# A transformer block on one Trainium2 core: two full expert pairs found among the first four batches and run beside the routing of the rest

## The chip, the cores and the metric

The kernel runs on one core of one Trainium2 chip. The metric is the device time of one execution in microseconds (us), the median of several; lower is better.

## The reference

Three stages, all in float32. Attention without a softmax on 8 batches, 8 heads, 576 tokens, head size 64; then a mixture of 8 experts that sends each of the 4608 tokens to its best expert; then a gated linear unit. Cut to its core:

```python
kv = np.einsum('bhsd,bhse->bhde', k, v)
out = np.einsum('bhsd,bhde->bhse', q, kv)
rms = np.sqrt(np.mean(out * out, axis=-1, keepdims=True) + 1e-06)
x = (out / rms * g_norm)                      # as tokens x 512
logits = x @ w_gate + modality_bias[modality_id]
e_idx = np.argmax(logits, axis=1)             # gate_w: softmax of the logits at e_idx
for e in range(8):                            # w1[e]: 512 x 1024, w2[e]: 1024 x 512
    mask = e_idx == e
    h = np.maximum(x[mask] @ w1[e], 0.0)
    out[mask] = gate_w[mask, None] * (h @ w2[e])
gate = 1.0 / (1.0 + np.exp(-(out @ w_gate2)))  # 512 x 1536
result = (gate * (out @ w_val)) @ w_out        # 1536 x 512
```

## The kernel before, in words

Every engine runs its instructions in the order in which the program emits them; the order is written out by hand. PE multiplies, DVE and ACT evaluate and split, POOL issues gathers and scatters, SP issues the other transfers. Float32 products are done as three products of split operands: ACT rounds a tile to a high part (`hi`), DVE subtracts it to get the residue (`lo`).

**Attention.** A loop over b = 0 to 8 (L397) computes batch b's `kv` products (`emit_kv`, into the matrix R) and transposed queries while it finishes batch b-1, in five steps r (`emit_out`, L290: the products of 128 tokens each, whose rows ACT copies and squares and whose squares DVE sums, L305). For b-2 it runs `norm` (L307: root mean square, and the logits). Batches go to the routing in pairs: `choose` (L330) takes the best expert, `rank` (L344) gives each token its place among the tokens of its expert, by ten small matmuls (L352 to L355) and a running total `tot` (L350), `lanes` (L371) and `numbers` (L378) make the one-hot tiles `lid` that carry token numbers, on POOL for the first two pairs of batches and on ACT (L385) for the others. `store_x` (L389) writes a batch's rows to `x_d` in DRAM through SP.

**Routing.** After the loop come the last `norm`, `choose`, `rank` and `lanes`, and then, on L478 to L548, the table of the whole: each expert's tokens are counted, cut into pair items of 256 tokens (18 of them) and single items of 128, and for each slot of 128 tokens the kernel finds the code (`sc`, L503), the token numbers by one-hot matmuls (`soh`, `php`, L508 to L520, giving `gidx`), the expert of each item (`est`, L524 to L531, which SP reads into registers) and the rows where results go (`sidx`, L533 to L548).

**Experts.** `run` (L925) goes through items 0 to 21, four steps each (j, a quarter of the hidden columns). A step: `emit_B` (24 matmuls with w1), the split of the next w1 quarter (`split_w`, L737), `emit_h` (ReLU and residue, L802 and L803), the split of the w2 quarter, `emit_D` of the step before (12 matmuls with w2). `gather` (L724) fetches the rows of an item from `x_d` by `gidx`, `norm_x` (L753) scales them, `emit_A` (L761) transposes them. Items alternate between two halves of a weight buffer; the pieces of item t+2 are loaded on SP as the pieces of item t have been split, under a register that skips the load where the expert is the same as two items before. Items 0 and 1 begin with expert 0, loaded ahead (L412, L451, L934, L935). `emit_y` (L839) scatters an item's result to `y_d`. `run` also unpacks float64 weights of the last stage (`Decode`, 28 units of 512 KB), one every 2.5 steps (L851), each loaded two steps before ACT takes its exponent (L129).

**The gated unit** (L1000 on) reads `y_d` and is bound by PE throughout. Its tiles `wos` (L1112) and `yr` (L1170) lie in pools of its own.

Of the kernel before, what the change touches and what calls it, by code (L numbers as in the profile page):

```python
# [1 line left out]

# [19 lines left out]
NT = B * S  # L22
# [11 lines left out]
NITEM = NPAIR + E  # L34
KC = DM // 128
# [47 lines left out]
def attention_moe_glu_kernel(  # L83
# [18 lines left out]
    est = const.tile([1, 2 * NITEM + 1], I32, name="est")  # L102

# [7 lines left out]
    class Decode:  # L111
# [34 lines left out]
        def store(self):  # L146
            m, cb, c = self.m, self.cb, self.c
            if m < 2:
                lo = (0, 128, 256, 384, 768, 896, 512, 640)[4 * m + c]
                nc.sync.dma_start(out=w_d[cb][:, :, lo:lo + 128], in_=self.f.rearrange("p (j f) -> p j f", f=128))  # L150
            else:
                nc.sync.dma_start(out=w_d[cb][:, c, 1024:1536], in_=self.f)

# [5 lines left out]
    with ExitStack() as st:  # L159
# [130 lines left out]
        def emit_out(b, r):  # L290
            if r == 0:
                o_t[b] = wk.tile([128, 4 + b % 2, XW], F32, tag=f"o{b % 2}", name="o", bufs=4 - b % 2)
# [85 lines left out]
        def numbers(bp, lo, act):  # L378

            t0, n, bc = 9 * bp, 9, [128, 9, 128]  # L380
            for w in range(2):
# [14 lines left out]

        for b in range(B + 1):  # L397
# [6 lines left out]
            for r in range(5):  # L404
                if b == B and r == 0:
# [4 lines left out]
                    w1r = [half0[:, 0].rearrange("p (c f) -> p c f", f=F1)]  # L410
                    w2r = [half0[:, 1].rearrange("p (c f) -> p c f", f=DM)]
                    nc.sync.dma_start(out=w1r[0], in_=w1[0].rearrange("(c p) f -> p c f", p=128))  # L412
# [15 lines left out]
                if r == 1:  # L428
# [6 lines left out]
                    for i in {6: (0, 1, 2), 7: (3, 4)}.get(b, ()):  # L435
                        store_x(i)
# [12 lines left out]
        norm(B - 1)  # L449
        store_x(B - 1)  # L450
        nc.sync.dma_start(out=w2r[0], in_=w2[0].rearrange("(c p) f -> p c f", p=128))  # L451
        numbers(2, lo, True)
        choose(3)
        lane = rank(3)


        tp = pkv.tile([128, 16], F32, tag="kv", name="totp")
        nc.tensor.matmul(out=tp[:, 0:8], lhsT=onesb, rhs=tot[:, 4, :], start=True, stop=True)
        for i in range(E):
            nc.tensor.matmul(out=tp[:, 8 + i:9 + i], lhsT=onesb, rhs=tot[:, 4, E - 1 - i:E - i], start=True, stop=True)  # L460
        numbers(3, lanes(3, lane), True)
        w1s = {(0, 0): [w1p.tile([128, KC, 256], F32R, tag="w1" + z, name="w1" + z) for z in "hl"]}
        wq = w1r[0][:, :, 0:256]
        nc.scalar.activation(out=w1s[0, 0][0], in_=wq, func=ACTF.Copy)
# [11 lines left out]
        soh = big.tile([128, NTILE, NSLOT], BF16, name="soh")  # L476
        item = ct[:, C_ITEM:C_ITEM + NITEM]
        nc.vector.tensor_scalar(out=ti, in0=tp, scalar1=127.0, scalar2=None, op0=ALU.add)  # L478
        nc.vector.tensor_scalar(out=ti, in0=ti, scalar1=7, scalar2=None, op0=ALU.arith_shift_right)
        nc.vector.tensor_scalar(out=tw[:, 0::2], in0=ti.rearrange("p (a e) -> p a e", a=2), scalar1=-2, scalar2=None, op0=ALU.bitwise_and)  # L480

        nc.vector.tensor_scalar(out=tw[:, 0, 0:1], in0=tw[:, 0, 0:1], scalar1=2.0, scalar2=None, op0=ALU.max)
        nc.vector.tensor_scalar(out=tw[:, 2, 7:8], in0=tw[:, 2, 7:8], scalar1=2.0, scalar2=None, op0=ALU.max)
        nc.vector.tensor_tensor(out=tw[:, 1], in0=ti[:, 8:16], in1=tw[:, 2], op=ALU.subtract)
        nc.vector.tensor_scalar(out=cums[0][:, :, 4:12], in0=tw[:, 0:2], scalar1=0.0, scalar2=None, op0=ALU.max)
        for i in range(3):
            nc.vector.tensor_tensor(out=cums[i + 1][:, :, 4:12], in0=cums[i][:, :, 4:12], in1=cums[i][:, :, 4 - 2 ** i:12 - 2 ** i], op=ALU.add)

        nc.vector.tensor_copy(out=seg[:, 0:9], in_=cums[3][:, 0, 3:12])
        nc.vector.tensor_scalar(out=seg[:, 9:10], in0=cums[3][:, 0, 11:12], scalar1=float(2 * NPAIR), scalar2=None, op0=ALU.max)  # L490
        nc.vector.tensor_scalar(out=seg[:, 10:18], in0=cums[3][:, 1, 4:12], scalar1=seg[:, 9:10], scalar2=None, op0=ALU.add)

        nc.vector.tensor_tensor(out=off, in0=ct[:, C_CODE:C_CODE + 18], in1=seg, op=ALU.subtract)
        nc.vector.tensor_tensor(out=off[:, 9:17], in0=off[:, 9:17], in1=tw[:, 2], op=ALU.add)
        nc.vector.tensor_tensor(out=dlt, in0=off[:, 1:18], in1=off[:, 0:17], op=ALU.subtract)
        bc = [128, NITEM, 17]
        nc.vector.tensor_tensor(out=cmp, in0=seg[:, 1:18].unsqueeze(1).broadcast_to(bc), in1=item.unsqueeze(2).broadcast_to(bc), op=ALU.is_le)
        nc.vector.tensor_tensor(out=cm2, in0=cmp, in1=dlt.unsqueeze(1).broadcast_to(bc), op=ALU.mult)
        nc.vector.tensor_reduce(out=itc, in_=cm2, op=ALU.add, axis=AX)
# [183 lines left out]
    with ExitStack() as st:  # L683
# [40 lines left out]
        def gather(t):  # L724
            if t >= end:
                return
# [605 lines left out]
```

## Time and profile before

| | |
|---|---|
| median of 3 runs | 1491.02 us (1490.17 to 1494.47) |
| profiled execution | 1496.44 us, its span 1494.7 us |
| mean granted clock of PE | 0.984 |
| PE, DVE, ACT, POOL busy, share of the span | 96%, 61%, 43%, 15% |
| HBM | 311.27 MB read, 68.63 MB written |

The span runs from the first to the last instruction on the core; the execution's own time has the launch around it. A busy PE counts pipelined matmuls, so durations of neighbouring matmuls overlap and the distance between their starts is the better price. A row of a timeline gives start and duration in us; "idle before" names what ended the wait. The granted clock is a share of full speed, 2.4 GHz.

### The profile page before, as it was taken

The page shows a single profiled execution, that of the slowest core. Times are in us where ns is not written, and L with a number is a line of the kernel's source. Part 1 is how long each engine was busy: PE and PEld are TensorE (multiplying, and loading weights), DVE is VectorE, ACT ScalarE, POOL GpSimd, SP SyncE. Part 2 cuts the span into 40 slices and gives each one's busy share as a digit, 9 for nine tenths or more (in the row PEclk, how much of TensorE's full clock was granted, in tenths as well). Part 3 has the DMA queues.
Part 4 walks back from the last instruction along what each step waited for, and adds up shares of the span by engine and source line. Part 5 has one row for each costly group of instructions (what it writes and reads, how often), then busy time and mean ns, then how long its engine had stood idle before and what let it go on. Part 6 is the DMA issues. An engine that isn't in the chain of part 4 may idle for free.

```text
span 1494.7 us, 22909 instructions
## 1 busy us (share of the span) xinstructions
PE 1429.6 (96%) x8633; PEld 1225.2 (82%) x8633; DVE 909.2 (61%) x1402; ACT 638.9 (43%) x1005; POOL 228.6 (15%) x302
## 2 busy tenths in 40 slices
PE   6984799999999999999999999999999999999997
PEld 6974689999999998778888887888888888888886
DVE  2557778788888877647876676343653436444442
ACT  3656455555555556746433342232322323221221
POOL 1011222222222221311011101010010200101011
PEclk9998799999999999999999999999999999999999
DMA  9975798858886766859886666556474564646444
GB/s 297 345 288 211 215 267 289 276 173 276 293 286 208 241 194 207 295 190 351 321 336 246 247 239 232 212 194 249 156 260 185 217 227 173 242 167 236 176 159 157
DMA packets 154979, 356.31 MB, mean 238 GB/s; under 512 B 20592, under 2 KB 74096, under 8 KB 147696
## 3 DMA queue, kind: packets, MB, share of 16 engines
q1 hardware_dynamic: 141872, 317.03, 61.0%
q0 software_dynamic: 11488, 36.27, 7.1%
q8 instruction: 71, 1.16, 0.3%
q10 hardware_dynamic: 1504, 1.48, 0.3%
q14 instruction: 44, 0.36, 0.1%
HBM read 311.27 MB, written 68.63 MB: 254 GB/s over the span
## 4 chain that ended last, share of the span: by engine, by line
PE 55%; DMA 1%; issue 0%; DVE 0%; POOL 0%; ACT 0%; POOLq 0%
PE gv L646 10%; PE gv L648 10%; PE gv L647 10%; PE ac L1163 6%; PE ac L1161 6%; PE ac L1162 6%; PE gv L620 1%; PE gv L621 1%; PE gv L622 1%; PE tr L583 1%; DMA wt_d<-wt 1%; POOL out_dram L1145 0%; DVE u L650 0%; POOLq L1328 0%; DVE wt L609 0%
## 5 line engine op out<-in xcount | busy, mean ns | idle before, releaser
L650 DVE TENSOR_TENSOR gm<-u,gv 128x512 f32<-128x512 f32 x96 | 65.9, 687 | 173.5 <-PE gv L648 172.3
L1161 PE MATMUL ac<-wos,gh 128*128 128x512 f32 x432 | 168.7, 390 | 0.0
L1163 PE MATMUL ac<-wos,gl 128*128 128x512 f32 x432 | 168.6, 390 | 0.0
L1162 PE MATMUL ac<-wos,gh 128*128 128x512 f32 x432 | 168.1, 389 | 0.0
L788 PE MATMUL ph<-xh,w1h 128*128 128x256 f32 x576 | 166.8, 290 | 0.8 <-ACT xh L771 0.8
L789 PE MATMUL ph<-xh,w1l 128*128 128x256 f32 x576 | 164.0, 285 | 1.2 <-DVE w1l L750 1.2
L790 PE MATMUL ph<-xl,w1h 128*128 128x256 f32 x576 | 164.1, 285 | 0.0
L670 ACT ACTIVATE s<-gv 128x512 f32<-128x512 f32 x48 | 28.8, 600 | 265.2 <-issue 207.7
L835 PE MATMUL py<-w2h,hh 128*128 128x512 f32 x304 | 119.3, 392 | 0.0
L836 PE MATMUL py<-w2l,hh 128*128 128x512 f32 x304 | 119.3, 392 | 0.0
L837 PE MATMUL py<-w2h,hl 128*128 128x512 f32 x304 | 118.5, 390 | 0.0
L646 PE MATMUL gv<-half,wt 128*128 128x512 f32 x288 | 113.3, 394 | 0.6 <-DVE u L650 0.6
L789 PEld LDWEIGHTS ph<-xh,w1l 128*128 128x128 f32 x576 | 111.3, 193 | 2.7 <-DVE w1l L750 1.4
L788 PEld LDWEIGHTS ph<-xh,w1h 128*128 128x128 f32 x576 | 111.2, 193 | 2.5 <-ACT xh L771 1.2
L648 PE MATMUL gv<-half,wt 128*128 128x512 f32 x288 | 112.5, 390 | 0.0
L647 PE MATMUL gv<-half,wt 128*128 128x512 f32 x288 | 112.1, 389 | 0.0
L790 PEld LDWEIGHTS ph<-xl,w1h 128*128 128x128 f32 x576 | 111.1, 193 | 0.3 <-DVE xl L772 0.3
L650 DVE TENSOR_TENSOR s<-u,gv 128x512 f32<-128x512 f32 x48 | 33.0, 688 | 118.3 <-PE gv L648 118.2
L1145 POOL DMA_INDIRECT out_dram<-ot,to x36 | 37.1, 1029 | 439.1 <-DVE ot L1142 190.4
L1163 PEld LDWEIGHTS ac<-wos,gl 128*128 128x128 f32 x432 | 81.1, 188 | 17.9 <-DVE gl L1130 0.4
L1162 PEld LDWEIGHTS ac<-wos,gh 128*128 128x128 f32 x432 | 81.1, 188 | 17.2
L1161 PEld LDWEIGHTS ac<-wos,gh 128*128 128x128 f32 x432 | 81.1, 188 | 17.0 <-ACT gh L1129 0.2
(275 smaller groups left out, 3323.7 us busy)
## 6 DMA issues: line engine op xcount, KB each, us to landing
wt<-wt_d SPq DMA_DIRECT2D x36, 1536.0 KB
wos<-wo_d SPq DMA_DIRECT2D x96, 512.0 KB
half<-in_moe_w_dram SPq DMA_DIRECT2D x88, 512.0 KB
w1r<-in_moe_w_dram SPq DMA_DIRECT2D x44, 512.0 KB
w2r<-in_moe_w_dram SPq DMA_DIRECT2D x44, 512.0 KB
rows<-w_d SPq DMA_DIRECT2D x24, 512.0 KB
wt<-wt_d SPq DMA_DIRECT2D x48, 256.0 KB
wt_d<-wt SPq DMA_DIRECT2D x12, 1024.0 KB
```

Of the source, the lines that this page charges most:

```text
L646: nc.tensor.matmul(out=o, lhsT=wh, rhs=yh[:, c, :], start=first and c == 0, stop=False, skip_group_check=True)
L647: nc.tensor.matmul(out=o, lhsT=wh, rhs=yl[:, c, :], start=False, stop=False, skip_group_check=True)
L648: nc.tensor.matmul(out=o, lhsT=wl, rhs=yh[:, c, :], start=False, stop=last and c == 1, skip_group_check=True)
L788: nc.tensor.matmul(out=o, lhsT=bh[:, c, cs], rhs=hi[:, c, 0:n], start=(c == 0), stop=False)
L789: nc.tensor.matmul(out=o, lhsT=bl[:, c, cs], rhs=hi[:, c, 0:n], start=False, stop=False)
L790: nc.tensor.matmul(out=o, lhsT=bh[:, c, cs], rhs=lo[:, c, 0:n], start=False, stop=(c == KC - 1))
L835: nc.tensor.matmul(out=o, lhsT=hi[:, f, cs], rhs=bh[:, f, :], start=first, stop=False)
L836: nc.tensor.matmul(out=o, lhsT=hi[:, f, cs], rhs=bl[:, f, :], start=False, stop=False)
L837: nc.tensor.matmul(out=o, lhsT=lo[:, f, cs], rhs=bh[:, f, :], start=False, stop=last)
L1161: nc.tensor.matmul(out=o, lhsT=gh[:, cs], rhs=wh, start=(k == 0), stop=False)
L1162: nc.tensor.matmul(out=o, lhsT=gh[:, cs], rhs=wl, start=False, stop=False)
L1163: nc.tensor.matmul(out=o, lhsT=gl[:, cs], rhs=wh, start=False, stop=(k == NJ - 1))
```

## The change

The functions of the expert stage move to the top of the kernel, with their tiles taken from whatever pool is set in `al`; the pool of x rows (`xp`) is open for the whole kernel. Then:

- In b = 6, step 2, `front_items` counts the tokens of each expert in batches 0 to 3, takes the first two full 256s in the order of the experts (`kd`: how many of them each expert gives) and writes their experts and codes.
- In b = 7, `front_rows` finds their token numbers by 36 one-hot matmuls, then the rows are gathered and SP reads the experts.
- In b = 8 the front's rows are scaled, transposed and split beside attention's last products. Item 0's weights are loaded by expert, in 8 pieces; item 1's pieces follow into the same half, if its expert differs.
- The eight steps of the two front items are emitted with the routing of the rest cut into pieces between them (`CHAIN`); `kd` takes the front's tokens out of the table, which now gives items 2 to 21. In step 6 the rows of items 2 and 3 are gathered and item 2's weights loaded. The scatter places follow the last step.
- Front results go to consecutive rows of `y_d` by a plain transfer.
- `run` begins with item 2; item 3's weights are loaded by SP at its start. One decode unit comes every 2.25 steps.
- Batches' row tiles have one buffer less (3 and 2), so `store_x` of batches 1, 0, 3 and 2 is emitted earlier. `wos` and `yr` use the tiles of `xp`.

The diff, cut to its core (the moved functions are otherwise as before):

```diff
+        def front_items():
+            ps = pq.tile([128, 8], F32, tag="q", name="tote")
+            nc.tensor.matmul(out=ps, lhsT=onesb, rhs=tot[:, 2, :], start=True, stop=True)
...
+            nc.vector.tensor_scalar(out=fi, in0=ps, scalar1=0.0, scalar2=None, op0=ALU.add)
+            nc.vector.tensor_scalar(out=fi, in0=fi, scalar1=8, scalar2=None, op0=ALU.arith_shift_right)
+            nc.vector.tensor_scalar(out=cue[0][:, 4:12], in0=fi, scalar1=0.0, scalar2=None, op0=ALU.max)
+            for i in range(3):
+                nc.vector.tensor_tensor(out=cue[i + 1][:, 4:12], in0=cue[i][:, 4:12], in1=cue[i][:, 4 - 2 ** i:12 - 2 ** i], op=ALU.add)
+            nc.vector.tensor_scalar(out=cf, in0=cue[3][:, 3:12], scalar1=float(NFRONT), scalar2=None, op0=ALU.min)
+            nc.vector.tensor_tensor(out=kd, in0=cf[:, 1:9], in1=cf[:, 0:8], op=ALU.subtract)
...
+            nc.vector.tensor_copy(out=est0, in_=ep[0:1])
+
+        def front_rows():
...
+            nc.vector.tensor_tensor(out=se, in0=sce.unsqueeze(1).broadcast_to(bc), in1=code[:, 0:n].unsqueeze(2).broadcast_to(bc), op=ALU.is_equal)
+            ps = pq.tile([128, 2, 2 * NFRONT], F32, tag="q", name="phe")
+            for w in range(2):
+                for t in range(n):
+                    nc.tensor.matmul(out=ps[:, w, :], lhsT=lid[:, t, w, :], rhs=se[:, t, :], start=(t == 0), stop=(t == n - 1))
+            nc.vector.tensor_scalar(out=ve, in0=ps[:, 0], scalar1=128.0, scalar2=-1.0, op0=ALU.mult, op1=ALU.add)
+            nc.vector.tensor_tensor(out=gidx0, in0=ve, in1=ps[:, 1], op=ALU.add)
...
-                    nc.sync.dma_start(out=w1r[0], in_=w1[0].rearrange("(c p) f -> p c f", p=128))
+                    for j in range(NJ1):
+                        load_w(0, j, 0)
+                        load_w(0, j, 1)
...
-                    for i in {6: (0, 1, 2), 7: (3, 4)}.get(b, ()):
+                    for i in {5: (1,), 6: (0, 3, 2), 7: (4,)}.get(b, ()):
                         store_x(i)
...
+                if b == B - 2 and r == 2:
+                    front_items()
+                if b == B - 1:
+                    if r == 2:
+                        front_rows()
+                    if r == 3:
+                        for t in range(NFRONT):
+                            gather(t)
+                    if r == 4:
+                        for t in range(NFRONT):
+                            read_item(t)
+                if b == B:
+                    if r in (1, 2):
+                        norm_x(0, r - 1)
+                    if r in (2, 3):
+                        emit_A(0, r - 2)
+                    if r == 3:
+                        split_w(0, 0, 0)
+                        load_w(1, 0, 0)
+                    if r == 4:
+                        split_w(0, 1, 0)
+                        load_w(1, 1, 0)
+                        split_w(0, 0, 1)
+                        load_w(1, 0, 1)
...
+        CHAIN = {0: [norm_last], 1: [lambda: numbers(2, lo, True, (0,)), lambda: choose(3), ranks],
+                 2: [lambda: numbers(2, lo, True, (1,)), totals, lanes3], 3: [segments, lambda: numbers(3, front.lo, True, (0,))],
+                 4: [slots, lambda: numbers(3, front.lo, True, (1,))], 5: [tokens], 6: [experts]}
+        steps = [(t, j) for t in range(NFRONT) for j in range(NJ1)]
+        for s, (t, j) in enumerate(steps):
+            emit_B(t, j)
+            for do in CHAIN.get(s, ()):
+                do()
+            emit_h(t, j)
+            if s == 6:
+                al.end = NSURE
+                for i in range(2):
+                    gather(NFRONT + i)
+            nt, nj = steps[s + 1] if s + 1 < len(steps) else (NFRONT, 0)
+            if nt < NFRONT:
+                split_w(nt, nj, 0)
+                if s and nt == 0:
+                    load_w(1, nj, 0)
+            split_w(t, j, 1)
+            if s and t == 0:
+                load_w(1, j, 1)
+            if s == 6:
+                for i in range(2):
+                    read_item(NFRONT + i)
+                for q in range(NJ1):
+                    load_w(NFRONT, q, 0)
+                    if q <= j:
+                        load_w(NFRONT, q, 1)
+            if s:
+                emit_D(*steps[s - 1])
+                if steps[s - 1][1] == NJ1 - 1:
+                    emit_y(steps[s - 1][0])
+            if t == 0:
+                if j in (0, 1):
+                    norm_x(1, j)
+                if j in (1, 2):
+                    emit_A(1, j - 1)
+        load_w(NFRONT, NJ1 - 1, 1)
+        for i in range(2):
+            norm_x(NFRONT, i)
+        split_w(NFRONT, 0, 0)
+        emit_D(*steps[-1])
+        for i in range(2):
+            emit_A(NFRONT, i)
+        emit_y(NFRONT - 1)
+        places()
...
-                at.setdefault((5 * i // 2 + d, what), []).append(i)
+                at.setdefault((9 * i // 4 + d, what), []).append(i)
...
-        run(0, NSURE)
+        run(NFRONT, NSURE)
```

## Rows read from the trace of the kernel before

**Rows 1.** The page, part 1: busy time, share, instructions of each engine.

```profile
PE 1429.6 (96%) x8633; PEld 1225.2 (82%) x8633; DVE 909.2 (61%) x1402; ACT 638.9 (43%) x1005; POOL 228.6 (15%) x302
```

**Rows 2.** Windows of 10 us: busy us (instructions), granted clock, DMA share, GB/s.

```profile
90.00:100.00 10.00, 6.56 (x142) 6.02 (x143) 5.08 (x17) 5.07 (x10) 1.36 (x3) 1.00 1.07 377
...
130.00:140.00 10.00, 1.69 (x21) 1.30 (x20) 8.82 (x29) 5.45 (x14) 0.21 (x1) 0.77 0.95 354
140.00:150.00 10.00, 0.90 (x19) 0.79 (x19) 8.97 (x38) 7.94 (x28) 0.22 (x1) 0.50 0.79 272
150.00:160.00 10.00, 2.80 (x72) 2.67 (x71) 9.08 (x34) 3.88 (x8) 3.38 (x4) 0.50 0.41 136
160.00:170.00 10.00, 8.34 (x37) 7.37 (x38) 4.25 (x6) 2.65 (x4) 4.59 (x5) 0.52 0.89 296
```

**Rows 3.** Timeline of PE: start, us, line, output<-inputs, count, idle before and its releaser.

```profile
122.57 1.23 PE L299 MATMUL ops<-R,qT 128*128 128x144 f32 x8
...
131.41 1.20 PE L299 MATMUL ops<-R,qT 128*64 128x144 f32 x16 [0.92 <-ACT o L301]
...
151.89 2.80 PE L512 MATMUL php<-soh,lid 128*128 128x44 bf16 x72 [8.42 <-DVE soh L508]
160.88 2.12 PE L767 MATMUL xtp<-ident,xg 128*128 128x128 f32 x8 [6.20 <-DVE sidx L548]
163.78 0.58 PE L788 MATMUL ph<-xh,w1h 128*128 128x256 f32 x1 [0.78 <-ACT xh L771]
...
212.08 0.28 PE L788 MATMUL ph<-xh,w1h 128*128 128x256 f32 x1
...
217.70 0.28 PE L788 MATMUL ph<-xh,w1h 128*128 128x256 f32 x1
```

**Rows 4.** Timeline of DVE around the routing.

```profile
110.71 0.17 DVE L350 TENSOR_TENSOR tot<-tot,tr 128x8 bf16<-128x8 bf16 x1
...
125.68 0.21 DVE L280 COPY R<-mp 128x64 f32<-128x64 f32 x1
...
130.38 0.17 DVE L314 TENSOR_SCALAR ssq<-ssq 128x32 f32<-128x32 f32 x1
...
138.07 0.18 DVE L314 TENSOR_SCALAR ssq<-ssq 128x40 f32<-128x40 f32 x1
...
142.55 0.28 DVE L349 TENSOR_REDUCE tr<-oh 128x8 f32<-128x72 bf16 x1
...
145.73 0.17 DVE L478 TENSOR_SCALAR ti<-totp 128x16 int32<-128x16 f32 x1
...
148.67 0.61 DVE L497 TENSOR_TENSOR cmp<-seg,ct 128x442 f32<-128x442 f32 x1
...
151.27 2.02 DVE L508 TENSOR_TENSOR soh<-sc,code 128x396 bf16<-128x396 bf16 x4
...
155.33 0.59 DVE L524 TENSOR_REDUCE esf<-cmp 1x26 f32<-1x442 f32 x1
...
157.02 0.44 DVE L533 TENSOR_TENSOR ex<-lg,mx 128x288 f32<-128x288 f32 x1
...
160.14 0.69 DVE L759 TENSOR_TENSOR xg<-xg 128x512 f32<-128x512 f32 x1
```

**Rows 5.** Groups of DVE, 220 to 600 us: busy us, mean ns, idle before.

```profile
L803 DVE SCALAR_TENSOR_TENSOR hl<-ph,hh 128x512 fp32r<-128x512 f32 x63 | 43.3, 688 | 25.2 <-ACT hh L802 25.2
L750 DVE TENSOR_TENSOR w1l<-half,w1h 128x1024 fp32r<-128x1024 f32 x34 | 41.5, 1222 | 2.5 <-ACT w1h L749 2.5
...
L772 DVE SCALAR_TENSOR_TENSOR xl<-xtp,gcol,xh 128x512 fp32r<-128x512 f32 x32 | 24.0, 751 | 24.7 <-ACT xh L771 21.0 <-issue 3.7
L759 DVE TENSOR_TENSOR xg<-xg 128x512 f32<-128x512 f32 x31 | 21.2, 684 | 0.0
```

**Rows 6.** Timeline of ACT: the lane products and a late decode piece.

```profile
138.43 5.35 ACT L385 ACTIVATE lid<-lo,ct 128x128 bf16<-128x128 bf16 x18
...
196.90 0.67 ACT L129 ACTIVATE d_e<-d_raw 128x512 f32<-128x512 f32 x1 [3.20 <-DMA d_raw<-in_moe_w_gate_dram]
```

More of the change, by code (lines that the diff above doesn't have):

```diff
@@ new lines, in part, with source, load_w @@
+    def part(t, j, which):
+        half = t % 2 if t >= NFRONT else 0
+        if which == 0:
+            return w1r[half][:, :, j * 256:j * 256 + 256]
+        return w2r[half][:, 2 * j:2 * j + 2, :]
+    def source(e, j, which):
+        if which == 0:
+            src = w1[bass.ds(e, 1), :, j * 256:j * 256 + 256]
+        else:
+            src = w2[bass.ds(e, 1), j * 256:j * 256 + 256, :]
+        return src.rearrange("o (c p) f -> p (o c) f", p=128)
+    def load_w(t, j, which):
+        if t < min(al.end, NSURE):
+            e, new = regs[t]
+            when = {} if new is None else dict(cond=new, cond_hint=False)
+            nc.sync.dma_start(out=part(t, j, which), in_=source(e, j, which), **when)
@@ new lines, in load_piece, with gather @@
+    def load_piece(t, j, which):
+        p = dec.tile([128, 1024], F32, tag="d_raw", name="d_raw", bufs=4)
+        src = source(regs[t][0], j, which)
+        p = p.rearrange("p (c f) -> p c f", f=src.shape[2])
+        nc.sync.dma_start(out=p, in_=src)
+        return p
+    xg_t, xT_t, hT_t, w2s, py_t = {}, {}, {}, {}, {}
+    def gather(t):
+        if t >= al.end:
+            return
+        for i in range(tiles_of(t)):
+            k = first_slot(t) + i
+            x = xp.tile([128, XW], F32, tag="xg", name="xg", bufs=4)
+            src, idx = (x_d[0:NT // 2, :], gidx0) if t < NFRONT else (x_d[:, :], gidx)
+            nc.gpsimd.indirect_dma_start(out=x, out_offset=None, in_=src,
+                                         in_offset=bass.IndirectOffsetOnAxis(ap=idx[:, k:k + 1], axis=0))
+            xg_t[t, i] = x
@@ new lines, in plain, with split_w @@
+    def plain(t, j, which=1):
+        return t >= NPAIR and which == 1 and j % 2 == 1
+    def split_w(t, j, which):
+        if t >= al.end or (t, j) in (w1s, w2s)[which]:
+            return
+        dst = (w1s, w2s)[which]
+        nm = f"w{which + 1}"
+        shape = [128, KC, 256] if which == 0 else [128, 2, DM]
+        src = load_piece(t, j, which) if t >= NSURE else part(t, j, which)
+        if plain(t, j, which):
+            dst[t, j] = (src, None)
+            return
+        hi, lo = al.w2() if which else [w1p.tile(shape, F32R, tag=nm + z, name=nm + z, bufs=3) for z in "hl"]
+        nc.scalar.activation(out=hi, in_=src, func=ACTF.Copy)
+        nc.vector.tensor_tensor(out=lo, in0=src, in1=hi, op=ALU.subtract)
+        dst[t, j] = (hi, lo)
@@ L496, in attention_moe_glu_kernel @@
[L496 to L499, printed above, removed]
-        nc.vector.scalar_tensor_tensor(out=itc, in0=itc, scalar=ct[:, C_CODE:C_CODE + 1], in1=item, op0=ALU.add, op1=ALU.add)
-        pairs = sc[:, 0:2 * NPAIR].rearrange("p (t i) -> p t i", i=2)
@@ L544, in attention_moe_glu_kernel, with ranks @@
[L544 to L548 removed]
+        def ranks():
+            front.lane = rank(3)
```

483 lines of the change are left out of this document (253 added, 230 removed).

## Prediction

> **What bounds the kernel now.** I read the page's totals first: PE is busy 1429.6 us of the span of 1494.7 [rows 1], so an edit pays only where PE stands still or is slow. The windows show where: from 130 to 160 us PE is busy 1.69, 0.90 and 2.80 us while DVE is busy 8.8 to 9.1, and the granted clock falls to 0.50, which is 1.2 GHz of the two levels [rows 2]. PE's timeline gives the edges: attention's last products run at 131.41 (1.20 us), the first transposes of gathered tokens at 160.88, the first expert product at 163.78 [rows 3]. Thus 31 us pass with hardly any PE work. DVE's timeline says what fills them: one unbroken chain, from batch 6's norm at 130.38, through norm and choice (138.07), rank and lanes (142.55), totals and segments (145.73), slots (148.67), one-hots (151.27), experts (155.33) and scatter places (157.02), to the first use of gathered tokens at 160.14 [rows 4]. The routing is serial work of small instructions on DVE, and the experts wait for all of it.
>
> **The yardstick.** Call T the moment at which the second product block of item 2 begins; by then both kernels have done the same expert work, items 0 and 1 whole and one block of item 2. It is 217.70 before [rows 3]. Behind it PE is full, so what T gains the end should gain. F is the moment of the first expert product, 163.78 before.
>
> **What comes first: does it find its pairs?** The reference's own arithmetic on its default inputs gives 442, 187, 206, 364, 209, 236, 367 and 293 tokens for the experts in batches 0 to 3. Experts 0, 3, 6 and 7 have full 256s, so the front items are expert 0 and expert 3. Over all batches there are still 18 pairs and 4 singles: no expert work is added. But items 2 and 3 are expert 0 again, in both halves, so its weights come twice more: I count 20 weight sets of 4 MB in place of 18.
>
> **F, step by step.** *Batch 6 of the loop.* The count of the front is a matmul behind rank's totals, ready at 110.88 [rows 4]; PE, in order, holds the next outputs and kv(7) behind it, about 1.4 us. Its 18 small DVE instructions cost (148.67 - 145.73) / 16 = 0.18 us each [rows 4], 3.3 us. DVE is not full there, so the copy that ends R of batch 7, at 125.68 [rows 4], moves by between 0 and 4.7 (3.3 + 1.4); I take 1.2, since DVE then mostly waits for PE's kv products: 126.9.
> *Batch 7.* The front's rows need a comparison (0.25), 36 matmuls and two additions (0.4). 72 such matmuls took 2.80 [rows 3], so 36 take 1.4; with the hand-overs the table stands at 129.5. They sit in PE's queue ahead of output (6,3), which began at 122.57 [rows 3] and now begins at 129.0. Two transposed tiles and two more outputs lie between it and batch 6's norm, 6.5 us by PE and ACT: norm at 135.5 in place of 130.38, 5.1 late (bounds: nothing, if PE's order hid it, and the 6.4 by which output (6,3) is late). This is the part of the change that costs.
> *The tail of attention.* Norm and rank take 4.6 (130.38 onwards, as the like of them at 138.07 and 142.55 do [rows 4]): 140.1. Then DVE has two sums of squares (512 columns like the scaling's, 0.7 each), lanes (1.3 of the 3.2 from 142.55 to 145.73), and, new, two scalings of gathered rows (0.68), two residues of x (0.75) and one of w1 (1.22) [rows 5], with 1.2 of waiting for ACT: 148.1. F is 148, 15.8 us before the old one. Without any of the delays of batches 6 and 7 it would be 142, with all of them at their upper bound 151.
>
> **From F to T.** A step of the expert pipeline (24 products, 12 second products) takes 217.70 - 212.08 = 5.62 us of PE [rows 3]. Nine first blocks and eight second ones are 8 x 5.62 + 2.85 = 47.8; four groups of transposes at 0.5 are 2.0; the routing's matmuls 2.8 + 0.9: 53.5. On DVE a step costs two residues of weights (1.22 each), one of h (0.69) and, in two steps of four, a scaling and a residue of x: 3.1 to 4.5 [rows 5]. The chain adds to steps 0 to 6 its pieces of 3.1, 3.2, 1.9, 3.0, 2.6, 2.6 and 1.7, and places (3.1) at the end [rows 4]. In steps 3 to 6 that makes 4.8 to 6.1, about what PE takes; in step 1 it is 7.7. Going through the queues in their order I find PE waiting five times: 2.8 for rank (the second block ends at F + 5.8, the choice at F + 8.5), 0.6 and 0.8 for split weights in steps 3 and 4, 1.3 for the residue of x ahead of item 2, 1.4 for places ahead of the next residue. That is 6.9: T = F + 60.4 = 208.4. ACT's lane products (5.35 per 18 [rows 6]) are spread at 2.7 over steps 1 to 4, where ACT has no more than its share of three copies and a transposed tile besides, and I let them fit.
> The gain is 217.70 - 208.4 = 9.3. Two more hand-overs of the kind that hl shows (25.2 / 63 = 0.4 [rows 5]) I take off: 8.5.
> PE's rate at F: the windows from 140 on, nearly empty, have 0.50, and the one from 90 to 100 us, with 6.56 busy, has 1.00 [rows 2]. PE before F is about half busy, so the first block may run at 1.2 GHz, 2.8 us more; PE waits 2.8 for rank right behind it, so it costs nothing.
>
> **What else moves, at nothing.** The conditional loads of item 1 sit in SP's queue ahead of the stores of batches 5 to 7; these are wanted only by the gather in step 6, some 35 us on, and the 4 MB of stores need 11 us at the 354 GB/s of [rows 2]. Item 3's weights (4 MB) queue on SP behind item 2's and ahead of the first decode piece, where POOL issued them before; they are due three steps later, 17 us against some 12. Decode pieces at every 2.25 steps in place of 2.5 add 0.1 us or so of DVE to a step with over 0.8 to spare. Later tiles that move to the pool of x rotate as before. Cover gone, each of these shows as a PE wait of some us at items 2 to 5.
>
> **Rivals.** *The routing hides better* (0.2). If DVE's slack takes the table of the front and PE's waits are half of mine, F is 144 and T 144 + 57 = 201: 17 gained, 1474. For it: DVE idles before 125, with 5.08 of 10 busy at 90 [rows 2]; against it: PE's order in batch 7.
> *Late transfers* (0.15). ACT waited 3.20 for a decode piece at 196.90 [rows 6], and the windows carry up to 377 GB/s [rows 2]. Items 2 and 3 now ask for 8 MB of weights beside some 3 MB of rows and decode in 23 us of PE, more than that rate gives; the 2 to 3 MB over take 7 us. If those fall on PE, 1 to 3 remain: 1489.
> *The queues serialise, slower* (0.11). Place: steps 0 to 7. If each piece of the chain adds its whole time to its step, since h waits on DVE behind a piece that waits for PE, T = F + 53.5 + 21.2 + 1.3 = 224.0: 6.3 lost, 1497. It decides once DVE has over 5.6 us in every step; by my sums it does in one or two. The Trainium skill (PSUM — Partial Sum Buffer, Engine vs sequencer instructions) has the queues of ScalarE and VectorE as strict FIFO, so a waiting piece holds all behind it; the trace agrees, with h's residue waiting 25.2 us in all for ACT.
> *The half clock stays* (0.04). If PE with its gaps runs the front at 1.2 GHz, 50 us of its work take 100: some 35 lost even with the waits hidden. Against it stands the window at 90. The Trainium skill (TensorE: Matmul & The Clock Gate, Part 1) calls the throttled state the default that activity lifts, which speaks against spreading PE's work over gaps; here the windows from 130 on show that default, the one at 90 does not.
>
> **How the numbers follow.** The profiled execution took 1496.44 us (span 1494.7), 5.4 above the median of 1491.02; the difference is carried to the median: 1491.0 - 8.5 = 1482.5. The forecast, 5 to 14 gained, holds 0.5. A measurement of this kernel tells about 0.3%, 4.5 us, from no change. Faster by that: 0.5 and 0.2 of the hiding rival, 0.70; the same: late transfers and a little of the forecast's edge, 0.16; slower: the last two with a margin for later stages, 0.14. The range for 8 in 10 reaches into the hiding case, to 1473, and over late transfers, to 1491; the slower cases stay out.
>
> **What would show it.** The first expert product at 145 to 151 us, the first output behind the front's rows near 129, item 2's second block near 208, granted clock 1.00 from 150 on, no gap of PE beyond 3 us between F and T. I am wrong if F is later than 155, if DVE is over 9.5 busy in every window from F to T with PE under 7, or if PE waits for weights between 200 and 260.

## The result, and the profile after

The changed kernel took **1504.72 us** (median of 4 runs, 1503.23 to 1513.22) against 1490.6 for the kernel before beside it (4 runs, 1487.29 to 1494.47): a ratio of 1.0106, 95% interval 1.0061 to 1.0151, so 15.8 us slower (9.1 to 22.5). The forecast was 1482.5 with a range to 1491. It was wrong, with the wrong sign; yet the front itself came out as forecast. The profiled execution took 1505.5 us, its span 1503.7.

The page's totals (first line), and windows of 10 us with PE, weight loads, DVE, ACT, POOL, then granted clock, DMA share, GB/s, answer to [rows 1, 2]:

```profile
PE 1448.7 (96%) x8670; PEld 1231.6 (82%) x8670; DVE 910.0 (61%) x1425; ACT 638.9 (42%) x1005; POOL 220.1 (15%) x304
...
140.00:150.00 10.00, 7.75 (x43) 6.93 (x44) 7.47 (x10) 6.56 (x9) 0.00 (x0) 0.67 0.65 218
150.00:160.00 10.00, 9.01 (x66) 8.28 (x65) 9.11 (x29) 5.83 (x14) 0.35 (x2) 0.92 0.94 330
160.00:170.00 10.00, 10.00 (x77) 9.10 (x77) 8.82 (x20) 9.07 (x24) 0.00 (x0) 1.00 0.99 363
...
220.00:230.00 10.00, 6.22 (x40) 5.18 (x37) 2.38 (x5) 3.14 (x5) 1.15 (x2) 1.00 1.05 361
230.00:240.00 10.00, 8.89 (x41) 8.26 (x42) 7.74 (x9) 4.12 (x6) 0.00 (x0) 0.66 0.75 69
240.00:250.00 10.00, 7.61 (x51) 6.61 (x51) 4.39 (x7) 4.73 (x7) 3.15 (x4) 1.00 1.04 385
```

The empty stretch is filled: PE has 7.75 and 9.01 where it had 0.90 and 2.80. A new hole stands at 220 to 250. And PE is busy 19.1 us longer in all with only 37 instructions more: somewhere the same products take longer. PE's timeline of the changed kernel gives the edges (as [rows 3]):

```profile
124.59 1.12 PE L615 MATMUL phe<-se,lid 128*128 128x4 bf16 x36 [3.35 <-DVE se L611]
125.57 2.27 PE L475 MATMUL ops<-R,qT 128*128 128x144 f32 x8
...
145.79 0.38 PE L266 MATMUL ph<-xh,w1h 128*128 128x256 f32 x1 [0.37 <-ACT w1h L227]
148.05 0.42 PE L267 MATMUL ph<-xh,w1l 128*128 128x256 f32 x1 [1.87 <-DVE w1l L228]
...
206.54 0.38 PE L266 MATMUL ph<-xh,w1h 128*128 128x256 f32 x1
...
210.85 0.39 PE L313 MATMUL py<-w2h,hh 128*128 128x512 f32 x1
...
229.20 0.38 PE L266 MATMUL ph<-xh,w1h 128*128 128x256 f32 x1 [3.36 <-ACT w1h L227]
231.11 0.58 PE L267 MATMUL ph<-xh,w1l 128*128 128x256 f32 x1 [1.52 <-DVE w1l L228]
...
246.51 0.38 PE L266 MATMUL ph<-xh,w1h 128*128 128x256 f32 x1 [0.94 <-ACT w1h L227]
...
248.34 0.39 PE L267 MATMUL ph<-xh,w1l 128*128 128x256 f32 x1 [1.45 <-DVE w1l L228]
...
251.18 0.39 PE L313 MATMUL py<-w2h,hh 128*128 128x512 f32 x1
...
653.17 0.47 PE L944 MATMUL gv<-half,wt 128*128 128x512 f32 x1 [0.30 <-PEq L1164]
```

F is 145.79, T is 206.54. The starts that answer to the last three edges in PE's timeline of the kernel before:

```profile
220.57 0.40 PE L835 MATMUL py<-w2h,hh 128*128 128x512 f32 x1
...
249.98 0.40 PE L835 MATMUL py<-w2h,hh 128*128 128x512 f32 x1
...
652.37 0.47 PE L620 MATMUL gv<-half,wt 128*128 128x512 f32 x1 [0.30 <-PEq L995]
```

So 9.7 us are gained at item 2 (210.85 for 220.57), all is lost by item 3's second block (251.18 for 249.98), 0.8 is lost at the first product of the gated unit, and the span ends 9.0 later. That is less than the runs show, since the profiled execution of the kernel before was 5.4 above its median. To compare executions whose attention differs, cut each span at these edges of PE's timeline: the last kv product, F, the first block of second products of item 2 and the second one of item 3, the first product of the gated unit, the end. The experiments are already in the table; their edits follow.

| us | to last kv | to F | to item 2 | items 2, 3 | other items | gated unit | span |
|---|---|---|---|---|---|---|---|
| before | 116.8 | 47.0 | 56.8 | 29.4 | 402.4 | 842.3 | 1494.7 |
| after | 115.3 | 30.5 | 65.1 | **40.3** | 402.0 | **850.6** | 1503.7 |
| e1 placement back | 114.1 | 29.3 | 65.0 | 43.2 | 399.6 | 846.5 | 1497.6 |
| e2 before, shifted | 106.4 | 47.3 | 55.7 | 29.1 | 397.9 | 851.2 | 1487.6 |
| e3 piece first | 113.3 | 30.2 | 65.0 | 42.0 | 402.5 | 851.5 | 1504.5 |
| e4 gate later | 119.6 | 29.2 | 65.1 | 37.1 | 402.0 | 849.8 | 1502.9 |
| e5 all three | 117.1 | 30.4 | 64.9 | 30.9 | 399.6 | 846.6 | 1489.6 |
| e6 pool right | 115.0 | 30.3 | 65.1 | 43.2 | 402.2 | 840.3 | 1496.2 |
| e7 decode later | 120.7 | 29.2 | 64.9 | 29.2 | 399.7 | 848.4 | 1492.0 |
| e8 both away | 117.1 | 30.3 | 65.1 | 29.4 | 402.3 | 842.9 | 1487.1 |
| e9 rows later | 116.8 | 29.8 | 65.1 | 29.4 | 402.3 | 840.4 | 1483.7 |
| e10 before, fewer row tiles | 111.1 | 47.7 | 56.3 | 29.4 | 402.3 | 846.3 | 1493.2 |
| e11 store sooner | 116.9 | 29.4 | 65.1 | 29.4 | 402.6 | 841.9 | 1485.2 |

From the last kv product to item 2 the change gains 103.8 - 95.6 = 8.2. Items 2 and 3 give back 10.9, the gated unit 8.3. Attention's own column varies by some 10 us between executions with PE's waits for loads, so it needs runs, not one profile.

**The hole at 220 to 250.** ACT's timeline of the changed kernel:

```profile
227.54 0.66 ACT L134 ACTIVATE d_e<-d_raw 128x512 f32<-128x512 f32 x1 [6.58 <-DMA d_raw<-in_moe_w_gate_dram]
228.11 1.04 ACT L227 ACTIVATE w1h<-w1r 128x1024 fp32r<-128x1024 f32 x1
...
244.83 0.68 ACT L134 ACTIVATE d_e<-d_raw 128x512 f32<-128x512 f32 x1 [4.68 <-DMA d_raw<-in_moe_w_gate_dram]
```

ACT stands 6.58 us for a decode piece, and the rounding of item 3's w1, for which PE waits at 229.20, stands behind it. Of the 10.9 us, 7.3 are the four waits of PE from 229.20 to 248.34. Behind the first two the granted clock is 0.66 from 230 to 240, and PE runs at its lower level: from 231.11 to 237.03 it takes 5.9 us for products that take 3.2 at 239.35, some 2.7 more. SP's queue says why the piece is late (start, time to issue):

```profile
209.19 2.39 SPq L190 DMA_DIRECT2D w1r<-in_moe_w_dram  x4
211.93 3.37 SPq L190 DMA_DIRECT2D w2r<-in_moe_w_dram  x4
215.36 0.46 SPq L128 DMA_DIRECT2D d_raw<-in_moe_w_gate_dram  x1
217.31 6.06 SPq L190 DMA_DIRECT2D half<-in_moe_w_dram  x3
223.48 0.41 SPq L1041 DMA_DIRECT2D gate_d<-gate  x1
223.93 3.02 SPq L1042 DMA_DIRECT2D gate_d<-gate  x1
...
231.69 0.46 SPq L128 DMA_DIRECT2D d_raw<-in_moe_w_gate_dram  x1
```

Item 3's 4 MB are issued first, and only from 209.19: SP had waited 9.5 us, and the profile ends that wait with the landing of item 1's results (`y_d`, which POOL issued at 204.93). The first piece (215.36) comes behind them. The second (231.69) is issued behind the store of the gate, 18 KB in pieces of 16 and 4 bytes (e4's expectation below calls all of them 4-byte pieces), while the transfers are 0.75 busy for 69 GB/s. That store is the same line of `run` as before, in its first step, but the first step is now item 2's. In the kernel before it ran at item 0 (SP from 180.88), and PE stayed full in that window, though ACT waited 3.20 at 196.90 [rows 6] for a decode piece issued right behind it:

```profile
180.00:190.00 10.00, 10.00 (x70) 9.22 (x69) 8.55 (x11) 4.91 (x7) 1.15 (x2) 1.00 0.81 61
```

The Trainium skill (DMA: Bandwidth & Descriptors, Why small descriptors are slow (HBM only)) gives every packet a fixed cost that small ones do not carry well; the trace agrees with its 0.75 and 0.81 busy for 69 and 61 GB/s.

**The gated unit.** PE's windows there, of the kernel before and of the changed one (PE busy and instructions, granted clock, DMA share, GB/s):

```profile
700.00:900.00 200.00, 200.00 (x901) 1.00 0.76 276
900.00:1100.00 200.00, 199.36 (x891) 1.00 0.57 212
1100.00:1300.00 200.00, 200.00 (x894) 1.00 0.58 215
```

```profile
700.00:900.00 200.00, 200.00 (x888) 1.00 0.77 277
900.00:1100.00 200.00, 199.42 (x881) 1.00 0.56 209
1100.00:1300.00 200.00, 200.00 (x888) 1.00 0.57 212
```

PE is full in both, at a granted clock of 1.00, and does 2657 products in place of 2686 in 600 us, 1.1% fewer. From start to start the products of `half` are 233 ns apart (median), 227 before. Neither a wait nor the clock explains that. What the change does move is addresses: its two small tables gidx0 and est0 take 32 bytes each, and the pool of x rows, 25,600 bytes, lies below everything else on the left side of SBUF.

### The profile page after: what moved, and what is told of

Read it like the earlier page. It is cut to its first block, busy times and chain, and to the rows that moved or that the text cites. A ratio compares the mean times of both kernels' runs of the same rounds, so it can differ in the third digit from the quotient of the medians.

```text
span 1503.7 us, 22996 instructions
## 1 busy us (share of the span) xinstructions
PE 1448.7 (96%) x8670; PEld 1231.6 (82%) x8670; DVE 910.0 (61%) x1425; ACT 638.9 (42%) x1005; POOL 220.1 (15%) x304
## 4 chain that ended last, share of the span: by engine, by line
PE 54%; DMA 4%; SPq 0%; issue 0%; POOL 0%; DVE 0%; ACT 0%; POOLq 0%; ACTq 0%
PE gv L970 10%; PE gv L972 10%; PE gv L971 10%; PE ac L1337 6%; PE ac L1335 6%; PE ac L1336 6%; DMA xg<-x_d,gidx 3%; PE gv L944 1%; PE gv L946 1%; PE gv L945 1%; PE tr L907 1%; DMA rows<-w_d 1%; DMA w_d<-d_f 0%; DMA y_d<-y,sidx 0%; SPq L1345 0%
## 5 line engine op out<-in xcount | busy, mean ns | idle before, releaser
L970 PE MATMUL gv<-half,wt 128*128 128x512 f32 x288 | 114.3, 397 | 0.6 <-DVE u L974 0.6
L972 PE MATMUL gv<-half,wt 128*128 128x512 f32 x288 | 113.7, 395 | 0.0
L971 PE MATMUL gv<-half,wt 128*128 128x512 f32 x288 | 113.6, 394 | 0.0
L313 PE MATMUL py<-w2h,hh 128*128 128x512 f32 x272 | 107.0, 393 | 0.0
L315 PE MATMUL py<-w2h,hl 128*128 128x512 f32 x272 | 106.7, 392 | 0.0
L314 PE MATMUL py<-w2l,hh 128*128 128x512 f32 x272 | 106.5, 392 | 0.0
```

The costliest lines, as they stand in the source:

```text
L313: nc.tensor.matmul(out=o, lhsT=hi[:, f, cs], rhs=bh[:, f, :], start=first, stop=False)
L314: nc.tensor.matmul(out=o, lhsT=hi[:, f, cs], rhs=bl[:, f, :], start=False, stop=False)
L315: nc.tensor.matmul(out=o, lhsT=lo[:, f, cs], rhs=bh[:, f, :], start=False, stop=last)
L970: nc.tensor.matmul(out=o, lhsT=wh, rhs=yh[:, c, :], start=first and c == 0, stop=False, skip_group_check=True)
L971: nc.tensor.matmul(out=o, lhsT=wh, rhs=yl[:, c, :], start=False, stop=False, skip_group_check=True)
L972: nc.tensor.matmul(out=o, lhsT=wl, rhs=yh[:, c, :], start=False, stop=last and c == 1, skip_group_check=True)
```

## The experiments

**e1: the 64 bytes taken back.**

```diff
-    gidx = const.tile([128, NSLOT], I32, name="gidx")
+    gidx_full = const.tile([128, NSLOT + 2 * NFRONT], I32, name="gidx")
+    gidx = gidx_full[:, 0:NSLOT]
...
-    gidx0 = const.tile([128, 2 * NFRONT], I32, name="gidx0")
-    est0 = const.tile([1, 4], I32, name="est0")
+    gidx0 = gidx_full[:, NSLOT:NSLOT + 2 * NFRONT]
+    est0 = sidx_full[0:1, NSLOT:NSLOT + 4]
```

> The changed kernel, with its two new small tables (gidx0, est0) laid into spare columns of two tables that were there before, so that every later tile on the left side of SBUF lies 64 bytes lower and stands to 128-byte lines as it did before the change; the computation is the same. Theory (placement): the gated unit's matmuls take 227 ns from start to start again in place of 230 to 233, and from 653 us on it takes 8 us less, as before the change; up to 650 us nothing changes, so the time is about 1496 against 1504.7. Rival (the tiles wos and yr in the pool of x, or other transfers, slow the gated unit): spacing stays at 230 to 233 and the time within 1 us of 1504.7.

Measured: median 1502.03 (10 runs), ratio to the kernel before 1.0075 (1.0053 to 1.0098). The gated unit took 846.5: half of the 8.3 came back, and the theory's 1496 was missed. The products of w1r and w2r stand mostly at 227 again, those of half at 227 to 231; those that read wos, in the pool of x, still stand at 231 and 229 (227 in the kernel before). So placement matters, and the offset within 128 bytes is not all of it.

**e2: the kernel before, shifted by 64 unused bytes.**

```diff
-    est = const.tile([1, 2 * NITEM + 1], I32, name="est")
+    est = const.tile([1, 2 * NITEM + 17], I32, name="est")[:, 0:2 * NITEM + 1]
```

> The kernel before, with 64 unused bytes behind the table est, so that every later tile on the left side of SBUF lies 64 bytes higher, as it does after the change; nothing else. Theory (placement): the gated unit's matmuls go from 227 to 230 to 233 ns apart, the gated unit takes some 8 us longer, the time is about 1499 against 1490.6, and nothing changes up to 652 us. Rival (not placement): the same time within 1 us.

Measured: 1489.37 (10 runs), ratio 0.9983 (0.996 to 1.0006). On the time the theory missed: not slower. On the stage it hit: the gated unit took 851.2, which is 8.9 more, with these windows:

```profile
700.00:900.00 200.00, 199.43 (x882) 1.00 0.73 266
900.00:1100.00 200.00, 200.00 (x887) 1.00 0.58 216
1100.00:1300.00 200.00, 200.00 (x889) 1.00 0.56 208
```

The expert items went the other way, 4.5 faster (397.9 for 402.4). 64 bytes that nothing reads move both stages by about 1%, in either direction. In this execution attention had none of PE's two waits for kv loads near 80 and 97 us (3.2 and 3.4 in the kernel before) and ended 10.4 earlier; whether the shift had a part in that is open. The two stages add up to 4.4 more, the runs show 2.5 less (6.0 less to 0.9 more), so other stages took less on the average too, and only the pace of the two stages is shown here.

**e3 and e4: the order of SP's queue.** e3 loads the first piece ahead of item 3's weights:

```diff
             if sure:
+                decode(0, "load")
                 for which in range(2):
...
-                if sure:
+                if sure and s:
                     decode(s, "load")
```

> The changed kernel, with the first decode piece loaded ahead of item 3's weights instead of behind them. Theory (order of SP's queue): ACT's wait of 6.6 us for that piece, which ended at 227.54 and stood in front of the rounding of item 3's w1, vanishes, and with it most of the 7.7 us lost between 223 and 236; the second wait (4.7 us, to 244.83) may stay. End about 1498. Rival (bandwidth: the same megabytes are due in the same time, whichever comes first): the wait moves to item 3's weights at the same place, and the time is within 2 us of 1504.7.

e4 stores the gate three items later:

```diff
-                if not s and sure:
+                if s == 12 and sure:
                     store_gate()
```

> The changed kernel, with the store of the gate (two transfers of 4-byte pieces that ran at 223 to 230) moved three items later. Theory (these pieces hold the queues: at 230 to 240 the transfers were busy for 0.75 of the time with only 69 GB/s): the second wait of ACT for a decode piece (4.7 us, to 244.83) falls below 1 us, 3 us are gained between 236 and 250, and the first wait stays at 6 to 7; the time is about 1501. Rival (the second piece is late because SP was blocked behind the first): the second wait stays at 4 to 5 and the time at 1504.

Measured: e3 1506.25 and e4 1504.68, one time each. In e3 the first wait is gone, but the second one has grown. ACT's timeline of e3:

```profile
218.54 0.66 ACT L134 ACTIVATE d_e<-d_raw 128x512 f32<-128x512 f32 x1
241.95 0.66 ACT L134 ACTIVATE d_e<-d_raw 128x512 f32<-128x512 f32 x1 [12.16 <-DMA d_raw<-in_moe_w_gate_dram]
```

In e4 the second wait is gone and the first one stays. ACT's timeline of e4:

```profile
231.18 0.66 ACT L134 ACTIVATE d_e<-d_raw 128x512 f32<-128x512 f32 x1 [7.07 <-DMA d_raw<-in_moe_w_gate_dram]
242.84 0.66 ACT L134 ACTIVATE d_e<-d_raw 128x512 f32<-128x512 f32 x1
```

e4's stretch is 37.1, 3.2 less, as its theory had it, and from 230 to 240 its transfers carry 370 GB/s in place of 69; the time does not show it, as attention ended 4.3 later in that execution. For e3 the rival's time came true, but not its reason: the wait moved to the next piece, behind the gate's store, not to weights. In e3 that piece was issued at 228.50, behind the gate's four transfers (220.02 to 226.09). Each edit alone leaves the other's wait.

**e5: both, with e1's placement** (the three edits above together).

> The changed kernel with three edits: the two small tables in spare columns (64 bytes back), the first decode piece loaded ahead of item 3's weights, the store of the gate three items later. Each second one of them alone left the other's wait. Theory (both waits have a cause of their own): no ACT wait for a decode piece above 2 us between 205 and 255, and the stretch from the second to the fifth second-product block behind item 2's start, 17.3 us in the kernel before and 28.3 with the change, takes at most 20; the time is about 1490. Rival (items 2 and 3 together ask for more than the transfers give, in whatever order): the stretch stays above 23, with waits for other transfers, and the time is about 1496.

Measured: 1490.72 (10 runs), ratio 1.0002 (0.9983 to 1.0021). Items 2 and 3 take 30.9; the expectation's three blocks, the last part of that stretch, take 18.9, with one wait of 3.42 left at 237.03. The time is where the theory put it, the wait above its 2 us. The same megabytes are due here as in the changed kernel, and most of the 10.9 us are gone: the rival falls.

**e7: decode begun six steps later** (with e1's placement and e4's edit).

```diff
-                at.setdefault((9 * i // 4 + d, what), []).append(i)
+                at.setdefault((2 * i + d + 6, what), []).append(i)
```

> The changed kernel with the two small tables in spare columns, the decode units begun six steps later (and one every 2 steps in place of 2.25, so that they end where they ended), and the store of the gate three items later: items 2 and 3 then have the transfers to themselves. Theory (too many megabytes are due at items 2 and 3): the stretch of three second-product blocks that took 28.3 us takes at most 19, no ACT wait for a decode piece above 2 us, and the end is some 11 us earlier than with the first edit alone: about 1490. Rival (item 3's weights are themselves late): PE waits for a weight tile of item 3 appear between 215 and 255, the stretch stays above 23, and the time above 1495.

Measured: 1489.03 (10 runs), ratio 0.9994 (0.9979 to 1.001). The stretch is 29.2, as before the change, its last three blocks 17.2; ACT waits for no piece there, and PE waits nowhere above 0.3 us between 213 and 600 us, though item 3's weights are still issued from 213.18. Its windows:

```profile
220.00:230.00 10.00, 10.00 (x64) 8.96 (x64) 7.06 (x8) 5.68 (x7) 1.15 (x2) 1.00 1.06 377
230.00:240.00 10.00, 10.00 (x67) 9.13 (x66) 5.64 (x7) 5.24 (x7) 2.14 (x2) 1.00 1.07 365
240.00:250.00 10.00, 10.00 (x73) 9.26 (x72) 7.17 (x8) 4.82 (x6) 4.17 (x4) 1.00 1.06 382
```

The transfers are full throughout and PE is too. So what cost 10.9 us was the decode and the gate store at the wrong moment; the weights fit. The time came as the theory had it, but its reason, too many megabytes, does not follow: e5 keeps the decode there and loses 1.5.

**e6: the pool of x rows at the other end of SBUF** (with e1's edit). Then every left tile has its old address, and only half0 lies 25,600 bytes lower; wos and yr stay in the pool of x.

```diff
-    xp = ctx.enter_context(tc.tile_pool(name="m_x", bufs=2, reuse_waits="tile"))
+    xp = ctx.enter_context(tc.tile_pool(name="m_x", bufs=2, side="right", reuse_waits="tile"))
```

> The changed kernel with the two small tables in spare columns and the pool of x rows at the other end of SBUF, so that every tile on the left side has the very address that it had before the change; only the tile half0 moves (by 25,600 bytes), and wos and yr still use the pool of x. Theory (addresses alone set the pace of the gated unit): matmuls whose moving operand lies on the left (w1r, w2r, rows) are 227, 227 and 231 ns apart as before the change, and only those that read half0 may differ; the gated unit takes at most 846 us against 850.6 and 842.3. Rival (wos and yr in the pool of x slow it): all of them stay at 229 to 232 and the gated unit at 846 to 851. Items 2 and 3 keep their loss.

Measured: 1497.97 (one time), the gated unit 840.3, 2 less than before the change. The medians from start to start are 227 ns for w1r, w2r and half, 228 to 234 for rows, and 227 for wos. PE's windows of e6:

```profile
700.00:900.00 200.00, 200.00 (x905) 1.00 0.78 281
900.00:1100.00 200.00, 199.36 (x891) 1.00 0.56 210
1100.00:1300.00 200.00, 200.00 (x894) 1.00 0.58 215
```

With the old addresses the old pace is back, to the instruction in two of three windows, while wos and yr still share a pool. The rival falls: the loss in the gated unit was placement alone. One profile of each kernel is enough for that, because a layout's pace repeats: from the 100th product of the gated unit to its end, e6, e8 and e10 keep the distance to the kernel before within 0.2 us, while the changed kernel falls back by 9.2.

**e8: both causes away** (e7 and e6 together) and **e9: the front's token numbers one step later in batch 7** (e8, and):

```diff
-                    if r == 2:
+                    if r == 3:
                         front_rows()
-                    if r == 3:
+                    if r == 4:
                         for t in range(NFRONT):
                             gather(t)
```

> The change with both causes of its loss taken away: the decode units and the store of the gate later, and the pool of x rows at the other end of SBUF so that the left side has its old addresses. Theory (these two are the whole loss, and what the front gains then reaches the end): the stretch of three second-product blocks takes 17 to 18, the gated unit 840 to 843, and the time is 7 to 10 below the kernel before: about 1482, which is what was forecast for the change itself. Rival (something else still takes it back): within 3 us of the kernel before.

> As the run before it, and the token numbers of the front found one step later in batch 7 (step 3, the gathers in step 4). Theory (PE's 3.4 us of waiting at these 36 matmuls is the cost of their place, and everything behind them in batch 7 waits too): the wait falls below 1 us, the stretch from the last kv product to the first expert product shrinks from 29 to 30 to some 27, and the time is 2 to 3 lower still. Rival (the gather of the front's rows becomes the bound of the first expert product): the wait goes, but the stretch stays at 29 or more.

Measured: e8 1486.01 (12 runs), ratio 0.9972 (0.9952 to 0.9992), 4.2 us gained (1.2 to 7.1); e9 1484.95, ratio 0.9969 (0.9947 to 0.9992). Behind the last kv product e8 stands as its theory says: 29.4 for items 2 and 3, 842.9 for the gated unit. But only half of the 8.2 arrives (at most 7.1 by the interval), so by these stages a third cause lies ahead of that edge. In e9 the place made nothing better: PE still waits 3.46 us at these matmuls, for `se` on DVE, and F comes 29.8 behind the last kv product. Its theory fell; the wait is on DVE's queue, not on the step.

**e10: the kernel before with the change's row tiles alone.** The prediction had no term for these: one buffer less for each tag, and the stores in another order. The profiles of e1, e3, e4, e7 and e9 show ACT waiting some 7 us between 97 and 104 us for a store to free a row tile. Those of the changed kernel itself, of e5, e6 and e8 do not; in them PE waits 3.7 to 4.0 near 96 us for a kv load.

```diff
-  o_t[b] = wk.tile([128, 4 + b % 2, XW], F32, tag=f"o{b % 2}", name="o", bufs=4 - b % 2)
+  o_t[b] = wk.tile([128, 4 + b % 2, XW], F32, tag=f"o{b % 2}", name="o", bufs=3 - b % 2)
...
-                    for i in {6: (0, 1, 2), 7: (3, 4)}.get(b, ()):
+                    for i in {5: (1,), 6: (0, 3, 2), 7: (4,)}.get(b, ()):
```

> The kernel before with one part of the change alone: one buffer less for the batches' row tiles (3 and 2), and the stores of batches 1, 0, 3 and 2 in the order that this asks for. Theory (this part costs attention 4 us: ACT's first copy of a late batch waits for a store to free its buffer, as it does for 7.2 us at 103 us in three runs of the changed kernel): that wait shows, the last kv product ends later, and the time is 3 to 5 above the kernel before. Rival (attention differs between executions by its waits for loads alone): the time within 1.5 us of the kernel before, and the wait either missing or taken up by the next wait for a load.

Measured: 1495.2 (10 runs), ratio 1.0038 (1.002 to 1.0056): 5.7 us lost (3.0 to 8.3). ACT's timeline of e10:

```profile
98.15 0.65 ACT L301 ACTIVATE o<-ops 128x576 f32<-128x576 f32 x1 [7.83 <-DMA x_d<-o]
```

Behind it PE's timeline of e10 has a wait:

```profile
99.99 0.19 PE L352 MATMUL rkp<-oh,ubf 128*128 128x72 bf16 x1 [4.30 <-ACT qT L287]
```

That this part of the change costs time is shown by the runs, and the rival's time, within 1.5 us, falls. That it costs it by this wait is not: in this one profile PE waits once near 80 to 100 us where the kernel before waits twice for loads (3.2 and 3.4), and attention ends 5.7 earlier. The expectation's "last kv product ends later" did not show.

Its gated unit has the old pace (901, 891 and 895 products in the three windows); the 4 us more of its last column lie ahead of them, in a longer wait for the first rows (3.63 at 668 us, 2.10 in the kernel before) and a granted clock of 0.97 from 600 to 700 us.

**e11: that store one batch sooner** (e9, and):

```diff
-                    for i in {5: (1,), 6: (0, 3, 2), 7: (4,)}.get(b, ()):
+                    for i in {4: (1,), 6: (0, 3, 2), 7: (4,)}.get(b, ()):
```

> As the run with both causes away and the token numbers one step later, and the store of batch 1, whose buffer batch 5 waits for, one batch earlier. Theory (the buffer is the wait): ACT's wait for that store is gone, and the time is 2 to 4 below that run's 1485, about 1482. Rival (the transfers are full there, and 1.3 MB put ahead of the loads delay the next kv products by as much): the same time within 1.5 us, with waits of PE for loads in its place.

Measured: **1481.72** (6 runs, 1476.18 to 1487.05), ratio 0.9935 (0.9912 to 0.9958): 9.7 us faster than the kernel before (6.3 to 13.1). ACT's wait for the store is gone, but the profiles of e5 and e8 have none either. This execution too had one of attention's waits for loads, so its first column does not show the gain; the runs do. The intervals of e9 and e11 overlap, so the theory's time came, but how much of the 5.1 us between them is this store stays open.

## Why the prediction was wrong

**Right: the bound, and the front as far as item 2.** F was put at 148 and came at 145.79, with its weight residue 1.87 late; T was put at 208.4 and came at 206.54. From F to T the sum said 60.4, the trace has 60.75. The transfers carried 364.7 MB in place of 356.4: two weight sets of 4 MB more, as counted. The table stood ready on DVE at 125.95 (forecast 129.5), batch 6's norm came at 134.58 (135.5). DVE's timeline, for [rows 4]:

```profile
124.19 0.21 DVE L456 COPY R<-mp 128x64 f32<-128x64 f32 x1
...
125.95 0.16 DVE L617 TENSOR_TENSOR gidx<-ve,phe 128x4 int32<-128x4 f32 x1
...
134.58 0.17 DVE L490 TENSOR_SCALAR ssq<-ssq 128x32 f32<-128x32 f32 x1
```

Attention's last kv product stood 1.5 earlier in this execution, which F and T both carry, and the copy of R was not delayed at all. Inside the totals several terms were off and made up for each other; that much is luck.
- *Batch 7.* The table came 3.4 early, yet from output (6,3) to batch 6's norm it took 9.0 (125.57 to 134.58) where 6.5 was put; the rows before have 7.8 (122.57 to 130.38 [rows 3, 4]). Behind PE's wait of 3.35 for `se` the granted clock was 0.72 from 120 to 130, where it was 1.00 before.
- *From F to T.* PE waited 4.6 where 6.9 was put: 1.87 and 0.46 for weight residues, 1.0 for the rank in place of 2.8, 1.28 ahead of item 2's first block, where 1.3 was put. The wait behind the places (1.09 for 1.4) came at 208.01, just behind T. The front's first block began at the lower of the clock's two levels (products 0.21 us apart up to 151.68, then 0.12; granted clock 0.67 and 0.92 in its windows). The sum had priced that at nothing, since the rank's wait would cover it; it took some 1.6 of the 2.3 that the waits left.

Counted from the last kv product the gain is 8.2; 8.5 was forecast. The serialised queues and the lasting half clock did not come.

**The step that failed: "What else moves, at nothing".** It listed item 3's weights, the first decode piece and the pool of x rows, and priced each at nothing.
- *The first piece behind item 3's weights.* The step said that the weights are due "three steps later, 17 us against some 12". It asked when the weights are due, not when the piece behind them is: ACT needs it two steps on, in front of the same weights' rounding. The rival of late transfers saw the place, "PE waits for weights between 200 and 260" was the named sign, but it left 1 to 3 us of gain; the stretch lost 10.9. Its reason, 2 to 3 MB too much for 23 us, was not the cause: e5 asks for the same megabytes in another order, without the gate's 18 KB, and loses 1.5; e7 moves the decode away and loses nothing.
- *The store of the gate* moves with `run`'s first step from item 0 into that stretch; its four transfers were not counted at all. e3, e4 and e5 show that both causes have to go: 42.0 and 37.1 with one of them left, 30.9 with none, against 40.3.
- *"Later tiles that move to the pool of x rotate as before"*, and before it *"Behind it PE is full, so what T gains the end should gain".* They rotate as before (e6), and PE is full; but a full PE has no fixed pace, and the addresses that the pool and 64 bytes move cost 8.3 us in the gated unit.

**The term that was missing: the row tiles.** With one buffer less, batch 5 takes the buffer of batch 1, whose store queues behind loads. The part alone, buffers and order of the stores together, costs 5.7 (3.0 to 8.3, e10). That the wait for this store is how it costs them is argued: six profiles with fewer row tiles show the wait and five do not, and in e10's profile attention ends earlier than before the change.

The account, in us: front -8.2, items 2 and 3 +10.9, other items -0.4, gated unit +8.3, row tiles +5.7: 16.3, against 15.8 measured (9.1 to 22.5). The first four are differences of one profile each and the last is from runs, so that they meet so closely is chance. Undone one after the other, with the front kept, the losses vanish: e11 gains 9.7 (6.3 to 13.1), where 8.5 was forecast for the change. The forecast priced the idea and not the moves that make room for it.

## What to carry to other kernels

When a stage is moved, list every transfer that its code issues, in the order of the queue, with the time at which each consumer asks for it: here a piece issued behind 4 MB but asked for before them, and an 18 KB store in small pieces, cost 10.9 us, and another order of the same megabytes gave 9.4 of them back. Buffers taken from one loop to make room for another are terms of the sum. And where PE is full for hundreds of us, compare its pace (instructions per window) before and after: a new tile far from the hot loop can move it by a per cent in either direction.

## What the runs showed of the hardware that was not expected

The pace of back-to-back 128x512 products depends on where their operands lie in SBUF: 227 ns from start to start at the old addresses (before, e6), up to 233 with 64 bytes of shift, at a granted clock of 1.00 each time; over the gated unit 840 to 852 us. The Trainium skill (SBUF — State Buffer, SBUF: two separate sides) says that TensorE never waits for another user of SBUF on the engine side; these runs do not say whom the slow products wait for, but their pace is not free of the layout. Which addresses collide is open: the offset within 128 bytes alone explains half (e1), and product by product the pattern repeats: between e3, e4 and the changed kernel, which share a layout, 96 to 99% of the distances in the gated unit agree within 2 ns, between the changed kernel and the kernel before 41%.
